# Cutting two value loads of the last head by partitions into 112, 8 and 8 rows, in a transfer-bound decode kernel

## The chip, the cores and the metric

The kernel runs on one core of a Trainium2 chip. The metric is the device time of one execution in microseconds (us). Every run here is in the fast state, and each time is a median; the kernel before was run beside every other kernel on the same chip. The three groups of experiments ran on three different chips; the kernel before differs by 0.07 us between them.

## The reference

One token of decode: layer norm, query projection, attention of 32 heads over a cache of 32,768 keys and values of 192 numbers each (bf16), output projection, then a small feed-forward block.

```python
def _A_ref(x, k_cache, v_cache, wq, wo):
    q = (x @ wq).reshape(B, Sq, 32, 192).transpose(0, 2, 1, 3)
    scores = jnp.einsum("bhqd,bhkd->bhqk", q, k_cache) * (192 ** -0.5)
    o = jnp.einsum("bhqk,bhkd->bhqd", softmax(scores), v_cache)
    return o.transpose(0, 2, 1, 3).reshape(B, Sq, 32 * 192) @ wo
h  = x + A(layernorm(x));   h2 = h + relu(layernorm(h) @ w1) @ w2     # shortened
```

Keys and values are 805 MB which must be read once. Everything else is small beside that.

## The kernel before

All large loads are issued by the sync engine to one queue, in the order in which they are used. A load puts a block of consecutive cache rows on each of 128 partitions:

```python
def load(dst, src, sem, *label):
    g.do(lambda: nc.sync.dma_start(out=dst, in_=src), sem, label, by=16)

def rows(src, h, k0, jl):
    return src[h, k0:k0 + P * jl, :].rearrange("(p j) d -> p (j d)", p=P)
```

The last head is loaded in smaller parts, so that little work is left after the last byte. Below, "the second value load" is the one marked (1), "the half-loads" are (2); J is 32, JL 64, Dh 192, P 128.

```python
        end_values(0, 0, JL * Dh, "dva", "v", LAST, 0)
        ...                                                    # keys
        end_values(1, 0, JL * Dh, "dvb", "v", LAST, 1)         # (1) 128 rows of 24,576 bytes
        ...                                                    # keys: 128 rows of 15,360, 6,144 and 3,072 bytes
        for i in range(2):                                     # (2) 128 rows of 12,288 bytes each
            end_values(2, i * J * Dh, (i + 1) * J * Dh, f"dvh{i}", "vh", i)
        ...                                                    # four last value pieces, wo, w1, w2 in four pieces
```

The softmax here doesn't subtract the row's maximum and nothing guards it: scores larger than these inputs give would overflow.

Of the kernel before, what the change touches and what calls it, by code (L numbers as in the profile page):

```python
# [80 lines left out]
def kernel(  # L81
# [13 lines left out]
    P = nc.NUM_PARTITIONS  # L95

    Bsz, Sq, D = A_x.shape
    _, H, Sk, Dh = A_k_cache.shape
# [9 lines left out]
    JL = 64  # L108
    J = 32
# [6 lines left out]
    LAST = H - 1  # L116
# [31 lines left out]
    v_hd = A_v_cache.rearrange("b h s d -> (b h) s d")  # L148
# [44 lines left out]
    for tag in ("ln1", "ln2"):  # L193
# [16 lines left out]
    v_at = {0: va[:, 0:JL * Dh], 1: va[:, JL * Dh:2 * JL * Dh], 2: va[:, 2 * JL * Dh:3 * JL * Dh],  # L210
            3: va[:, 0:40 * Dh], 4: va[:, 40 * Dh:56 * Dh], 5: va[:, 56 * Dh:64 * Dh]}
# [8 lines left out]
    def v_tile(h, ld):  # L220
        return v_at[ld] if h == LAST else va[:, ld * JL * Dh:(ld * JL + JK) * Dh]
# [11 lines left out]
    def dma_program(g):  # L233
# [6 lines that stand above are left out]
        def keys(h, ld):  # L240
            if h > 0:
                g.wait("PV", h - 1, 4 * ld)
                g.wait("scs", h - 1, 4 * ld + 3)
            elif ld == 1:
                g.wait("att0")
            load(kt[ld][:], rows(k_hd, h, P * JK * ld, JK), f"dk{ld}", "k", h, ld)

        def vals(h, ld):
            if ld == 1:
                g.wait("PV", h, 1)  # L250
            elif h > 0:
                g.wait("PV", h - 1, 5)
            load(v_tile(h, ld), rows(v_hd, h, P * JK * ld, JK), ("dva", "dvb")[ld], "v", h, ld)

        for c in range(DT):
            load(wq_c[c], wq_view[:, c * H * Dh:(c + 1) * H * Dh], f"dwq{c}", "wq", c)
        for h in range(LAST):
            for ld in range(NK):
                keys(h, ld)
                vals(h, ld)  # L260
            if h % 2 == 0 and h < LAST - 1:
                if h > 0:
                    g.wait("prj", h)
                load(wo_s[:], wo_view[h // 2], "dwo", "wo", h // 2)

        def end_keys(i, k0, jl, sem):
            load(k_at[i], rows(k_hd, LAST, k0, jl), sem, "k", LAST, i)

        def end_values(ld, c0, c1, sem, *label):
            load(v_at[ld][:, c0:c1], rows(v_hd, LAST, P * JL * ld, JL)[:, c0:c1], sem, *label)  # L270


        g.wait("PV", LAST - 1, 0)
        g.wait("scs", LAST - 1, 3)
        end_keys(0, 0, JL, "dk0")
        end_keys(1, P * JL, JL, "dke0")
        g.wait("PV", LAST - 1, 3)
        end_values(0, 0, JL * Dh, "dva", "v", LAST, 0)
        g.wait("PV", LAST - 1, 4)
        g.wait("scs", LAST - 1, NC - 1)  # L280
        end_keys(2, 2 * P * JL, JL, "dk1")
        g.wait("PV", LAST - 1, 5)
        end_values(1, 0, JL * Dh, "dvb", "v", LAST, 1)
        k0 = P * JL * (NL - 1)
        at = []
        for i, jl in enumerate(ENDJ):
            at.append((k0, jl))
            end_keys(NL - 1 + i, k0, jl, f"dke{1 + i}")
            k0 += P * jl
        g.wait("PV", LAST - 1, NC - 1)  # L290
        for i in range(2):
            end_values(2, i * J * Dh, (i + 1) * J * Dh, f"dvh{i}", "vh", i)
        i = 0
        for ld, (k0, jl) in enumerate(at):
            for c, (l, off, jc, *_) in enumerate(ends):
                if l == NL - 1 + ld:
                    g.wait("PV", LAST, 1)
                    load(v_tile(LAST, l)[:, off * Dh:(off + jc) * Dh],
                         rows(v_hd, LAST, k0, jl)[:, off * Dh:(off + jc) * Dh], f"dve{i}", "vc", LAST, c)
                    i += 1  # L300
        g.wait("prj", LAST - 1)
        load(wo_s[:], wo_view[H // 2 - 1], "dwo", "wo", H // 2 - 1)
        g.wait("PV", LAST, 3)
        load(w1_s, B_w1.rearrange("(c p) n -> p c n", p=P), "dw1", "w1")
        for i, (c0, c1) in enumerate(zip(W2_CUTS[:-1], W2_CUTS[1:])):
            load(w2_s[:, c0:c1], B_w2.rearrange("(c p) n -> p c n", p=P)[:, c0:c1], f"dw2_{i}", "w2", i)
# [451 lines left out]
    for f in (dma_program, pool_program):  # L758
        f(plan)
# [58 lines left out]
    with nc.Block(name="decode_blk", no_gpsimd_drain=True) as block:  # L818
        @block.sync
        def _(eng):  # L820
            dma_program(Program(book, sems, nc.sync))

        @block.gpsimd
        def _(eng):
            pool_program(Program(book, sems, nc.gpsimd))

        @block.scalar
        def _(eng):
            looped("act", nc.scalar)

        @block.vector
        def _(eng):
            looped("dve", nc.vector)

        @block.tensor
        def _(eng):
            looped("pe", nc.tensor)
# [34 lines left out]
```

## Time and profile before

| | before |
|---|---|
| time, median of 4 | 1914.89 us (1914.77 to 1914.92) |
| busy share of the load queue | 99.8% of 16 engines' span |
| mean rate | 431 GB/s |
| row of 24,576 bytes on one transfer engine | 0.912 us |
| last landing, and end of the profiled span | 1909.35 and 1912.9 us |

In the views PE is the matmul engine, PEld its weight loads, DVE and ACT the vector and scalar engines, POOL is GpSimd and SP the sync engine. The page's views give shares of the span by engine and in 40 slices, the queues, and the chain of waits that ended last. The packet records of the same trace give start, duration and size of each transferred row; I take row durations from there. A full transfer leaves sixteen marks at its landing (the last one's lie within 2.8 us); I take them as one for each of the sixteen engines, and a transfer as landed at its last mark. The lines of the kernel before are shown in the prediction.

### The profile page before, as it was taken

Reading aid. Unit: us, or ns where it says so; the run is one execution under the profiler, and the core shown is the slowest. Engines: PE = TensorE matmul, PEld = TensorE weight load, DVE = VectorE, ACT = ScalarE, POOL = GpSimd, SP = SyncE. Lnnn points to the kernel's source line nnn. Section 1 sums busy time; section 2 is a strip of 40 time slices with the busy share of each in tenths; the row PEclk is TensorE's granted clock in tenths of the full one; section 3 lists DMA queues with packets and bytes.
Section 4 is the critical chain, followed back from the end, with each engine's and each line's share of the span. In section 5 each row is a group of like instructions: output and inputs, shape, how many; then the busy total and the mean of one; then the engine's idle time right before and its main releaser. Section 6 shows DMA issues by size and latency. Waiting matters only on the chain.

```text
span 1912.9 us, 35974 instructions
## 1 busy us (share of the span) xinstructions
PE 1580.2 (83%) x15908; PEld 1000.8 (52%) x15908; DVE 1559.8 (82%) x731; ACT 938.7 (49%) x2001; POOL 1.0 (0%) x6
## 2 busy tenths in 40 slices
PE   7778888888888788888888887878888788888888
PEld 7455455554554555545545545545455455555555
DVE  2787887987878878789788888888798887987887
ACT  2454454554544535545445445455354454553554
POOL 0000000000000000000000000000000000000000
PEclk9988898898898998988989989989889899898899
DMA  9999999999999999999999999999999999999999
GB/s 409 436 433 431 435 432 435 431 439 432 435 432 435 436 430 436 432 436 430 439 432 436 431 436 431 438 432 436 432 435 432 435 433 434 435 430 441 431 429 372
DMA packets 25185, 825.28 MB, mean 431 GB/s; under 512 B 2635, under 2 KB 4172, under 8 KB 7628
## 3 DMA queue, kind: packets, MB, share of 16 engines
q1 hardware_dynamic: 25152, 824.98, 99.8%
q8 instruction: 15, 0.25, 0.0%
q14 instruction: 6, 0.05, 0.0%
q10 hardware_dynamic: 12, 0.00, 0.0%
HBM read 824.97 MB, written 0.00 MB: 431 GB/s over the span
## 4 chain that ended last, share of the span: by engine, by line
DMA 70%; PE 28%; SPq 1%; ACT 1%; issue 0%; POOLq 0%; DVE 0%
DMA va<-in_A_v_cache_dram 69%; PE o_ps L354 25%; PE sp L354 2%; SPq L235 1%; ACT kT L577 1%; PE mm L354 1%; DMA kt<-in_B_w_dram 0%; PE tp L373 0%; POOLq L336 0%; PE attT L354 0%; PE mm L566 0%; ACT pB L583 0%; ACT y_row L639 0%; ACT pA L592 0%; DVE y_col L753 0%
## 5 line engine op out<-in xcount | busy, mean ns | idle before, releaser
L663 DVE TENSOR_TENSOR pr<-kt,qb 128x2304 f32<-128x2304 bf16 (+2 forms) x257 | 755.9, 2941 | 315.3 <-POOLq L317 293.9
L577 ACT COPY kT<-tp 128x1024 bf16<-128x1024 bf16 (+1 forms) x899 | 814.9, 1019 | 286.6 <-PE tp L373 286.5
L666 DVE TENSOR_REDUCE sc<-pr 128x12 f32<-128x2304 f32 (+2 forms) x257 | 755.3, 2939 | 8.9
L354 PE MATMUL o_ps<-va,pB 128*2 128x384 bf16 x2306 | 500.0, 371 | 181.8 <-POOLq L336 147.5
L373 PE MATMUL tp<-ident_f,kt 128*128 128x128 f32 x3459 | 518.5, 288 | 122.7 <-ACT kT L577 75.9
L373 PEld LDWEIGHTS tp<-ident_f,kt 128*128 128x128 f32 x3459 | 380.7, 144 | 222.4 <-ACT kT L577 168.6
L354 PEld LDWEIGHTS o_ps<-va,pB 128*2 128x2 bf16 x2306 | 198.2, 91 | 405.3 <-POOLq L336 152.9
L354 PE MATMUL o_ps<-va,pA 128*2 128x384 bf16 x1790 | 370.6, 352 | 0.0
L592 ACT ACTIVATE pA<-sc 128x12 bf16<-128x12 f32 (+2 forms) x257 | 59.0, 229 | 529.6 <-DVEq L65 529.6
L354 PEld LDWEIGHTS o_ps<-va,pA 128*2 128x2 bf16 x1790 | 161.9, 90 | 173.0 <-issue 54.3
L354 PEld LDWEIGHTS sp<-qm,kT 128*128 128x128 bf16 x6918 | 197.1, 97 | 76.5 <-ACT pB L583 28.4
L354 PE MATMUL sp<-qm,kT 128*128 128x2 bf16 x6918 | 212.6, 164 | 16.2 <-ACT pB L583 13.4
L583 ACT ACTIVATE pB<-sp 128x20 bf16<-128x20 f32 (+2 forms) x258 | 61.4, 238 | 113.0 <-PE sp L354 112.9
L583 ACT ACTIVATION_READ_ACCUMULATOR pB<-sp 128x1 f32 x258 | 64.0, 248 | 0.0
L592 ACT ACTIVATION_READ_ACCUMULATOR pA<-sc 128x1 f32 x257 | 52.9, 206 | 0.0
L354 PE MATMUL o_ps<-xn_ln,kt 128*96 128x1 bf16 (+1 forms) x316 | 22.3, 208 | 2.6 <-DMA kt<-in_A_wq_dram 2.5
L354 PEld LDWEIGHTS o_ps<-xn_ln,kt 128*96 128x96 bf16 (+1 forms) x316 | 22.2, 176 | 2.7 <-issue 2.6
L678 DVE TENSOR_SCALAR o_pair<-o_ps,rec 2x384 bf16<-2x384 f32 x32 | 19.4, 605 | 1.5 <-PE o_ps L354 0.4
L354 PEld LDWEIGHTS attT<-oT,wo_s 128*128 128x128 bf16 x465 | 13.6, 96 | 10.3 <-issue 9.9
L354 PE MATMUL attT<-oT,wo_s 128*128 128x1 bf16 x465 | 16.3, 164 | 0.3 <-DVE oT L688 0.3
L354 PEld LDWEIGHTS mm<-dsums,ones_mat 128*128 128x128 f32 x64 | 9.5, 188 | 10.9 <-issue 10.3
L612 ACT CAST qe<-o_ps 96x64 bf16<-96x64 f32 x1 | 0.2, 208 | 27.5 <-PE o_ps L354 27.5
(65 smaller groups left out, 141.3 us busy)
## 6 DMA issues: line engine op xcount, KB each, us to landing
kt<-in_A_k_cache_dram SPq DMA_DIRECT2D x62, 6144.0 KB, 33.4
va<-in_A_v_cache_dram SPq DMA_DIRECT2D x62, 6144.0 KB, 21.0
kt<-in_A_k_cache_dram SPq DMA_DIRECT2D x3, 3072.0 KB, 24.6
wo_s<-in_A_wo_dram SPq DMA_DIRECT2D x16, 480.0 KB, 15.0
kt<-in_A_wq_dram SPq DMA_DIRECT2D x4, 1536.0 KB, 10.8
va<-in_A_v_cache_dram SPq DMA_DIRECT2D x2, 3072.0 KB, 31.0
va<-in_A_v_cache_dram SPq DMA_DIRECT2D x2, 1536.0 KB, 34.8
kt<-in_A_k_cache_dram SPq DMA_DIRECT2D x1, 1920.0 KB, 30.1
```

The source lines that it names most:

```text
L235: g.do(lambda: nc.sync.dma_start(out=dst, in_=src), sem, label, by=16)
L354: return lambda: pe.matmul(o, lhsT=w, rhs=r, **kw)
L373: calls.append(lambda b=b, o=o: pe.transpose(out=dst[:, b, :], in_=src[:, o:o + 2 * P].bitcast(f32), identity=ident_f[:]))
L577: g.do(lambda: act.copy(out=kT[c % 2][:, b0:b0 + nb, :], in_=src[:, 0:nb, :].bitcast(bf16)), "act_pe", ("cp", h, c, k))
L583: g.do(lambda: act.activation(out=pB[c % NB][:, 0:jp], in_=sp[:, 0:jp], func=F.Exp, scale=SCALE, accum_out=dsums[:, 2 * c + 1:2 * c + 2]), ...
L592: g.do(lambda: act.activation(out=pA[c % NB][:, 0:jd], in_=sc[c % NC][:, 0:jd], func=F.Exp, scale=SCALE, accum_out=dsums[:, 2 * c:2 * c + ...
L612: g.do(lambda: act.copy(out=qe[:], in_=o_ps[0:HE, 0:2 * H]), "act_pe", ("qe",))
L663: g.chain(lambda: dve.tensor_tensor(out=pr[:, 0:j1 - j0, :], in0=src[:, (off + j0) * Dh:(off + j1) * Dh].rearrange("p (j d) -> p j d", d=D ...
L666: g.chain(lambda: dve.reduce_sum(out=sc[c % NC][:, j0:j1], in_=pr[:, 0:j1 - j0, :], axis=X), "dve")
L678: g.do(lambda: dve.tensor_scalar_mul(out=o_pair[:, :, 1, :], in0=o_ps[0:2, 0:2 * Dh].rearrange("q (i d) -> q i d", i=2), scalar1=rec[0:2, ...
```

## The change

If the rows of every load are dealt out evenly, which is the author's premise, all engines' lists are equally long in bytes. Yet the engines do not end together: the marks of the last transfer are spread over 2.8 us. The change is meant to give eight engines, here called 0 to 7, one row more and the others, 8 to 15, one fewer of load (1) and of the first load (2), by cutting off two pieces of eight rows each: 112 rows are counted as seven for each of sixteen engines, a piece as one for each of eight. The traces bear no engine numbers, but they show eight marks for each piece: the page counts 2,667 packets under 512 bytes, the marks among them, after the change and 2,635 before, 32 more for four pieces.

```diff
-        def end_values(ld, c0, c1, sem, *label):
-            load(v_at[ld][:, c0:c1], rows(v_hd, LAST, P * JL * ld, JL)[:, c0:c1], sem, *label)
+        def end_values(ld, c0, c1, sem, *label, cuts=(0, P)):
+            for i, (p0, p1) in enumerate(zip(cuts[:-1], cuts[1:])):
+                load(v_at[ld][p0:p1, c0:c1], rows(v_hd, LAST, P * JL * ld, JL)[p0:p1, c0:c1], sem,
+                     *(label if p1 == P else label + ("part", i)))
+
+        HALF = (0, P - 16, P - 8, P)
...
-        end_values(1, 0, JL * Dh, "dvb", "v", LAST, 1)
+        end_values(1, 0, JL * Dh, "dvb", "v", LAST, 1, cuts=HALF)
...
-            end_values(2, i * J * Dh, (i + 1) * J * Dh, f"dvh{i}", "vh", i)
+            end_values(2, i * J * Dh, (i + 1) * J * Dh, f"dvh{i}", "vh", i, cuts=HALF if i == 0 else (0, P))
```

## The prediction

Port is the author's word here, and in the expectations, for a place in the on-chip memory at which rows of several engines wait for each other. That there are such places was a supposition when this was written. That a row of a piece waits with three others is the premise of the estimates for that case: four times the measured row of 0.912 or 0.460 us.

> **What bounds the kernel now.** I read the page first: busy share by slice, the queues, and the chain that ended last.
>
> ```profile
> PE   7778888888888788888888887878888788888888
> ...
> DMA  9999999999999999999999999999999999999999
> GB/s 409 436 433 431 435 432 435 431 439 432 435 432 435 436 430 436 432 436 430 439 432 436 431 436 431 438 432 436 432 435 432 435 433 434 435 430 441 431 429 372
> ...
> q1 hardware_dynamic: 25152, 824.98, 99.8%
> ...
> DMA 70%; PE 28%; SPq 1%; ACT 1%; issue 0%; POOLq 0%; DVE 0%
> ```
>
> The transfer engines are full in every slice and one queue keeps all sixteen busy for 99.8% of the span, while PE is at 83%. So the time is the time in which the slowest transfer engine empties its list, plus what follows its last byte. The windows of the last head show how near the end that holds (columns: window, its length, busy us and instruction count of PE, weight loads, DVE, ACT, POOL, then granted clock, transfer share, GB/s):
>
> ```profile
> 1860.00:1880.00 20.00, 18.30 (x232) 12.43 (x231) 19.27 (x11) 15.85 (x36) 0.00 (x0) 1.00 0.99 423
> 1880.00:1900.00 20.00, 19.58 (x173) 11.12 (x170) 19.04 (x9) 9.24 (x27) 0.00 (x0) 1.00 1.01 421
> 1900.00:1913.00 13.00, 7.23 (x153) 5.74 (x152) 2.44 (x14) 2.34 (x6) 0.00 (x0) 0.64 0.63 239
> ```
>
> Transfers are saturated until about 1907. Next PE's timeline at the end and the chain in order of time:
>
> ```profile
> 1898.59 1.46 PE L354 MATMUL o_ps<-va,pB 128*2 128x384 bf16 x8 [0.20 <-DMA va<-in_A_v_cache_dram]
> ...
> 1906.99 0.94 PE L354 MATMUL attT<-h1T,kt 128*128 128x1 bf16 x30 [0.75 <-DMA kt<-in_B_w_dram]
> 1908.20 0.56 PE L354 MATMUL attT<-h1T,kt 128*128 128x1 bf16 x15 [0.27 <-DMA kt<-in_B_w_dram]
> 1909.03 0.66 PE L354 MATMUL attT<-h1T,kt 128*128 128x1 bf16 x15 [0.27 <-DMA kt<-in_B_w_dram]
> ```
>
> ```profile
> 1899.56 9.43 DMA kt<-in_B_w_dram
> 1908.98 0.05 issue
> 1909.03 0.67 PE attT L354 x15
> ```
>
> The last value piece, then every piece of w2, is awaited by PE. The last landing is the end, less some 3.5 us of fixed tail (1909.35 to 1912.9). Whatever delays the slowest transfer engine delays the end one for one.
>
> The page does not tell the engines apart, but the trace records sixteen landing marks per transfer. For the last one (last w2 piece) they lie at 1906.54 plus 0, 0.28, 0.69, 0.73, 0.80, 1.12, 1.21, 1.26, 1.35, 1.43, 2.51, 2.62, 2.65, 2.70, 2.72, 2.81 us: ten early engines and six late ones. For the second value load of the last head (mark 1873.59) thirteen lie within 1.43 us and three at 2.65 to 2.83. The pattern is nearly constant from 200 us on, because no engine ever empties: an engine that falls behind stays behind. It changes near instruction blocks: the records show 16,384-byte packets of 0.88 to 0.96 us on the instruction queue at 1865.5, 1875.1, 1887.5 and 1902.2, and after each one more engine lies about 1.3 us later. That is the unevenness which the change would trade against.
>
> [...] The trace shows an engine's own rate (24,576 bytes in 912 ns, 26.9 GB/s) but, with every load spread evenly, nothing of ports shared by engines.
>
> **The change part by part.** No compute instruction moves: the order of PE, DVE, ACT and POOL is the same, and no byte is added. The sync queue has four more issues at 0.33 to 0.43 us each, 1.5 us at most. They are hidden: in the profile it stands blocked at its issues (13.57 us at one of w2) [...]. Four more completion marks at 9 ns each on engines 0 to 7 are nothing.
>
> Rows: a row of the second value load is 24,576 bytes, 912 ns; a row of the first half-load 12,288 bytes, 460 ns. Engines 0 to 7 get one more of each, +1.37 us. Engines 8 to 15 get one fewer of each, -1.37 us.
>
> If all engines run freely, the new end is the larger of (latest of engines 0 to 7, +1.37) and (latest of 8 to 15, -1.37). I cannot see which numbers the six late ones bear. If even one of the latest is in the lower half the end is 1.2 to 1.4 us later. If all six are in the upper half, the lower half is eight of the ten early ones, whose latest is at 1.26 to 1.43; plus 1.37 gives 2.63 to 2.80 against 2.81 now, a gain of 0 to 0.2 us. So with free engines the time is -0.2 to +1.4 us, most likely +1.3: the swap of 2.74 us between the halves overshoots the gap of about 1.3 us, and there was little to win.
>
> If instead the port limits[...]. Four rows through a port take 4 x 0.912 = 3.65 us, not 0.91. Two pieces of the value load take 7.3 us, in place of the one row (0.91) that those engines lose from the 128-row load: +6.4 us. The half-load likewise: 2 x 4 x 0.46 = 3.7 for 0.46, +3.2 us. Sum +9.6 us on engines 0 to 7[...]. It may be more: [...] 5/4 of 7.3 + 3.7 = 13.8, +12.4. The 112-row load may also collide[...]. It is less where the ports have reserve or the collisions overlap with waiting of others. Of the end this makes +8 to +13 us: the transfers before the end are never idle, so nothing hides it, but if the slowest engines were in the upper half up to 2.8 us of their lag is absorbed.
>
> **The rivals.** (a) Free engines, -0.2 to +1.4 us, 1914.7 to 1916.3. For it: [...] no trace here shows a shared port. [...] I give it 35%. (b) Ports shared, +8 to +13 us, 1923 to 1928; 45%. Between both, partial sharing, +2 to +8 us; 15%. (c) A true gain: the late engines are all upper ones and each step waits for them. At most the earlier landing of the six late ones, about 1.3 us, 1913.6; against it the overshoot above; 5%. [...] (e) Compute becomes the bound: PE reaches each awaited piece with 0.2 to 0.75 us of slack, so a gain over about 0.7 us would not pass to the end, and a loss passes fully.
>
> **Range and chances.** Weighted: 0.35 x 0.9 + 0.45 x 10 + 0.15 x 5 - 0.05 x 0.7 = 5.5 us, so 1920.4; the possibilities are in two heaps and I choose the middle between rather than one. The range from 1914.2 to 1927.5 covers (a), the part of (b) up to the estimate with fifth shares, and a bit of gain. Two per cent is 38 us, far outside of all this: within 2% has 0.98.
>
> **What would show it.** Right on shares: the value load's and half-load's small rows last about four times 912 and 460 ns in the packet records, or the landings of the eight-row pieces spread over microseconds; the GB/s of the slices at 1870 to 1890 falls under 400; PE's waits on values and w2 grow by microseconds. Right on free engines: rows keep 912 and 460 ns, and eight landing marks of the last piece move by +1.37 and eight by -1.37 against the others. Wrong altogether if the marks keep their old pattern [...], or if the time falls by over 1 us: then the late engines are the upper eight and the overshoot argument fails.

## The result, and the profile after

The changed kernel takes 1934.21 us (1931.83 to 1937.63 over four runs), against 1914.89. The ratio is 1.0102, with a 95% interval of 1.0085 to 1.012. A ratio here is the mean time of one kernel's fast runs over that of the other's in the same rounds, so it is not quite the ratio of the medians. The change costs 19.3 us. Predicted were 5.5 us (1920.4, with a range up to 1927.5), and within that 8 to 13 us, an estimate, for the case that engines share ports. By the measure of 2% it counts as the same.

The page of the changed kernel, the lines on transfers and the chain:

```profile
DMA  9999999999999999999999999999999999999998
GB/s 415 433 427 434 433 435 433 433 433 433 436 433 433 433 432 436 433 433 433 433 436 433 431 433 434 433 436 431 433 433 434 436 431 433 434 433 437 430 342 283
...
q1 hardware_dynamic: 25184, 824.98, 99.8%
...
DMA 71%; PE 27%; SPq 1%; issue 0%; POOLq 0%; ACT 0%; DVE 0%
```

The busy shares say nothing: the load queue is at 99.8% in both kernels. Only the rate in the last two slices has dropped, from 429 and 372 to 342 and 283 GB/s. So the time by which rows are slowed counts as busy. The windows of the last head show it better (same columns as in the prediction):

```profile
1840.00:1860.00 20.00, 19.38 (x167) 11.57 (x167) 18.68 (x10) 8.34 (x18) 0.00 (x0) 0.93 1.00 433
1860.00:1880.00 20.00, 18.34 (x212) 11.88 (x212) 18.08 (x10) 14.41 (x34) 0.00 (x0) 0.83 1.07 294
1880.00:1900.00 20.00, 10.96 (x72) 5.92 (x72) 16.24 (x8) 3.82 (x11) 0.00 (x0) 0.74 0.94 230
1900.00:1920.00 20.00, 13.48 (x107) 7.05 (x107) 4.00 (x3) 6.95 (x22) 0.00 (x0) 0.83 1.00 352
```

Up to 1860 us nothing differs. Then the transfer share stays about 1 while the rate halves, from 421 to 230 GB/s in the window from 1880 to 1900, and PE's busy time there falls from 19.58 to 10.96 us. PE's timeline shows for what it waits (start, duration, operation, number; in brackets the idle time before it and what ended it):

```profile
1889.04 3.36 PE L358 MATMUL o_ps<-va,pB 128*2 128x384 bf16 x10 [9.11 <-POOLq L340]
...
1906.99 3.36 PE L358 MATMUL o_ps<-va,pB 128*2 128x384 bf16 x10 [6.40 <-DMA va<-in_A_v_cache_dram]
...
1928.58 0.70 PE L358 MATMUL attT<-h1T,kt 128*128 128x1 bf16 x15 [0.28 <-DMA kt<-in_B_w_dram]
```

The first wait is that for the second value load, handed on by GpSimd, which here only relays its landing; the load landed at 1888.94 us. The second is that for the first half-load, whose last mark is at 1906.94 us. The chain in order of time agrees:

```profile
1851.36 37.59 DMA va<-in_A_v_cache_dram
1888.94 0.03 issue
...
1918.02 10.52 DMA kt<-in_B_w_dram
1928.53 0.05 issue
1928.58 0.72 PE attT L358 x15
```

The last landing moves from 1909.35 to 1928.94 us, and the span from 1912.9 to 1932.5: the tail after the last byte keeps its 3.6 us. So the loss lies wholly in the transfers. Here are the rows behind it, from the packet records:

| rows | before, mean us | after, mean us | extra time per engine (rows x difference / 16) |
|---|---|---|---|
| second value load, 128 rows | 0.912 | 1.999 | 8.7 us |
| keys behind it, 128 rows of 15,360 bytes | 0.579 | 0.979 | 3.2 us |
| both half-loads, 256 rows | 0.462 | 0.811 | 5.6 us |

Together they make 17.5 of the 19.6 us by which the last landing moved. The rest is not resolved by this count; engines also end less evenly, over 4.6 us instead of 2.8.

### The profile page after: what moved, and what is told of

Read it like the earlier page. It is cut to its first block, busy times and chain, and to the rows that moved or that the text cites. A ratio compares the mean times of both kernels' runs of the same rounds, so it can differ in the third digit from the quotient of the medians.

```text
span 1932.5 us, 35978 instructions
## 1 busy us (share of the span) xinstructions
PE 1583.9 (82%) x15908; PEld 992.3 (51%) x15908; DVE 1559.8 (81%) x731; ACT 937.5 (49%) x2001; POOL 1.0 (0%) x6
## 2 busy tenths in 40 slices
DMA packets 25217, 825.28 MB, mean 427 GB/s; under 512 B 2667, under 2 KB 4204, under 8 KB 7660
## 3 DMA queue, kind: packets, MB, share of 16 engines
q1 hardware_dynamic: 25184, 824.98, 99.8%
## 4 chain that ended last, share of the span: by engine, by line
DMA 71%; PE 27%; SPq 1%; issue 0%; POOLq 0%; ACT 0%; DVE 0%
DMA va<-in_A_v_cache_dram 70%; PE o_ps L358 24%; PE sp L358 2%; SPq L235 1%; DMA kt<-in_B_w_dram 1%; PE mm L358 1%; POOLq L340 0%; PE tp L377 0%; PE attT L358 0%; PE mm L570 0%; ACT y_row L643 0%; DVE y_col L757 0%; SPq L871 0%; SPq L152 0%
## 5 line engine op out<-in xcount | busy, mean ns | idle before, releaser
L358 PE MATMUL o_ps<-va,pB 128*2 128x384 bf16 x2306 | 508.5, 375 | 199.0 <-POOLq L340 157.7
L377 PE MATMUL tp<-ident_f,kt 128*128 128x128 f32 x3459 | 512.3, 284 | 120.8 <-ACT kT L581 79.3
L377 PEld LDWEIGHTS tp<-ident_f,kt 128*128 128x128 f32 x3459 | 370.9, 142 | 225.5 <-ACT kT L581 175.3
L675 DVE TENSOR_REDUCE rec<-mm 128x1 f32<-128x20 f32 x32 | 5.7, 179 | 21.6 <-PE mm L358 17.1
```

Source lines behind the costliest of these rows:

```text
L358: return lambda: pe.matmul(o, lhsT=w, rhs=r, **kw)
L377: calls.append(lambda b=b, o=o: pe.transpose(out=dst[:, b, :], in_=src[:, o:o + 2 * P].bitcast(f32), identity=ident_f[:]))
L675: g.chain(lambda: dve.reduce_sum(out=rec[:, 0:1], in_=mm[:, 0:2 * NCM], axis=X), "dve")
```

## The experiments

**Theory.** The loads fill the 128 partitions of the on-chip memory. It is supposed that a row waits when another engine writes to partitions that share a port with its own, and that this happens in loads of another shape than 128 rows (rows of 1.999 us in the mean in the changed kernel's second value load), not in a 128-row load (0.912 us). Which partitions share one is for the runs to show: adjacent ones against ones four apart, and the lower 64 against the upper 64. **Rivals.** The uneven lists (nine rows against seven) set the end; each extra transfer costs; the read side, memory, is what collides.

The first two edits are shown against the changed kernel, the others against the kernel before, with the cutting function of the change in place. Twelve kernels ran:

| run | the second value load as | time, us | loss against before of the same rounds |
|---|---|---|---|
| e1_even | 112 and 16 rows; first half-load too | 1931.56 | 16.8 |
| e2_first_only | 112, 8 and 8 rows | 1926.49 | 11.8 |
| e3_halves64 | 64 and 64 rows | 1925.23 | 10.5 |
| e4_columns | three thirds of the columns, 128 rows each | 1914.86 | 0.1 |
| e5_adjacent8 | 16 pieces of 8 adjacent rows | 1945.23 | 30.4 |
| e6_step8 | 16 pieces of 8 rows, 4 partitions apart | 1931.21 | 16.4 |
| e7_adj_to | as e5, source rows four apart | 1952.86 | 38.1 |
| e8_adj_from | as e6, source rows adjacent | 1931.05 | 16.2 |
| e9_seven_apart | 7 times 16 rows, 7 partitions apart; 16 rows | 1925.49 | 10.7 |
| e10_first_even | 112 and 16 rows | 1925.61 | 10.8 |
| e11_adjacent16 | 8 pieces of 16 adjacent rows | 1930.11 | 15.3 |
| e12_shift | 7/8 of the columns whole, 1/8 as 16 pieces of 8 rows, 4 apart | 1917.27 | 2.5 |

The kernel before took 1914.74, 1914.81 and 1914.80 us in the three groups of rounds (e1 to e4, e5 to e8, e9 to e12).

**Are uneven lists the cause?** The first run keeps the 112-row part but gives every engine eight rows.

```diff
-        HALF = (0, P - 16, P - 8, P)
+        HALF = (0, P - 16, P)
```

> Both loads as 112 and 16 rows: every transfer engine keeps eight rows, nobody has nine or seven. Ports theory [...]: the 112-row part stays as slow as in the changed kernel (rows of the second value load 1.5 to 1.8 us instead of 0.91), [...] about two thirds of the loss stays, 1925 to 1932 us. Theory of uneven lists (nine rows against seven delay the end): the loss is gone, 1915 us.

It took 1931.56 us, ratio 1.0091 (1.0074 to 1.0108). With even lists 16.8 of 19.3 us stay, so unevenness is not the main cause. The rows of the 112-row part of the second value load took 1.73 us in the median, as long as in the changed kernel (1.74).

**How much does each load carry?**

```diff
-            end_values(2, i * J * Dh, (i + 1) * J * Dh, f"dvh{i}", "vh", i, cuts=HALF if i == 0 else (0, P))
+            end_values(2, i * J * Dh, (i + 1) * J * Dh, f"dvh{i}", "vh", i)
```

> Only the second value load is cut, the half-load is whole again. Ports theory: the loss follows the bytes that are cut, so two thirds of 19.3 us, about 12 to 13 us, 1927 us. A fixed cost per extra transfer would make it half, 1924.5 us. Uneven lists: 0.92 us of 1.37 us, 1915.8 us.

It took 1926.49 us: 11.8 of 19.3 us, 61%, with the larger of the two cut loads, which has two thirds of their bytes. The remaining 39%, 7.5 us, comes with the half-load. This is nearer to a cost by bytes than to one by transfers, which would be half, but the spread of the changed kernel (5.8 us) is too wide to rule out a mixture by this run alone. The control tests the cost by transfers alone:

```diff
-        end_values(1, 0, JL * Dh, "dvb", "v", LAST, 1)
+        for i in range(3):
+            end_values(1, i * 64 * JL, (i + 1) * 64 * JL, "dvb", *(("v", LAST, 1) if i == 2 else ("v", LAST, 1, "col", i)))
```

> Control: the second value load is cut into three by columns, each with all 128 partitions, so there are as many extra transfers as in the first cut of the change. Ports theory: no collision, 1915 us (within 0.5). A cost per extra transfer, or of shorter runs in memory: several us more.

It took 1914.86 us, ratio 1.0 (0.9984 to 1.0017). Two more transfers and rows a third as long cost nothing that shows. So it is the partitions of a transfer that matter, not the number of transfers.

**Is half of the partitions written at half the rate?**

```diff
-        end_values(1, 0, JL * Dh, "dvb", "v", LAST, 1)
+        end_values(1, 0, JL * Dh, "dvb", "v", LAST, 1, cuts=(0, P // 2, P))
```

> Only the second value load is cut, into partitions 0 to 63 and 64 to 127: four rows an engine from each half, lists even. Ports theory: [...] its 64 rows need 64 x 0.912 / 8 = 7.3 us and the pair 14.6 instead of 7.3 us; rows near 1.82 us each, time 1922 us. Uneven lists or a cost per transfer: 1915 us.

It took 1925.23 us, ratio 1.0053 (1.0036 to 1.007). The windows from 1868 to 1874 us, within the load, of the control by columns and then of this run:

```profile
1868.00:1874.00 6.00, 5.74 (x59) 3.79 (x58) 4.35 (x5) 2.63 (x7) 0.00 (x0) 0.82 1.00 421
```

```profile
1868.00:1874.00 6.00, 3.05 (x40) 2.94 (x39) 5.67 (x6) 1.50 (x6) 0.00 (x0) 0.82 0.98 205
```

The engines are equally busy and move half as much, 205 against 421 GB/s. Rows took 1.89 us in the median; twice 0.912 is 1.82. The loss is larger than the 7.3 us expected (the estimate was half of the partitions at half the rate): eight rows an engine at 1.87 (mean) instead of 0.91 make 7.6 us, and the keys behind it were slowed too, eight rows at 0.83 instead of 0.58, 2.0 us. That engines still at the value load hold them up is my guess; this run does not show it.

**Write side or read side?** The next four runs use 16 pieces of eight rows. The rows of a piece lie on eight adjacent partitions or on eight that are four apart. Destination and source are then exchanged.

```diff
-        end_values(1, 0, JL * Dh, "dvb", "v", LAST, 1)
+        ADJ = [slice(8 * i, 8 * i + 8) for i in range(P // 8)]
+        STEP = [slice(32 * b + r, 32 * b + r + 29, 4) for b in range(P // 32) for r in range(4)]
+        eights(ADJ, ADJ)     # its definition is left out: one load for each pair of slices; (destination, source): e6 (STEP, STEP), e7 (ADJ, STEP), e8 (STEP, ADJ)
```

> Second value load as 16 pieces of eight adjacent rows, half-load whole. [...] Ports theory: [...] 16 pieces 58 us instead of 7.3, so about 1965 us. Uneven lists alone: engines 0 to 7 have 16 rows instead of eight, +7.3 us, 1922 us.

It took 1945.23 us (1941.65 to 1946.88).

> The same 16 pieces of eight rows on engines 0 to 7, but the rows of a piece are four partitions apart[...]. Ports theory: no two rows of a piece collide; 16 x 0.912 = 14.6 instead of 7.3 us [...]: 1922 to 1930 us, some 35 us or more under adjacent rows. Uneven lists or a cost per transfer: the same time as adjacent rows.

It took 1931.21 us (1929.46 to 1932.62). Same number and size of pieces and, by the premise, the same engines and lists, 14.0 us less, though 35 us or more were expected. (The upper end of the expected range, 1930 us, is an estimate for the case that the other eight engines get in the way of some pieces.) Two windows of this run:

```profile
1868.00:1874.00 6.00, 5.84 (x60) 3.86 (x58) 4.09 (x5) 2.78 (x12) 0.00 (x0) 0.86 1.01 422
1876.00:1882.00 6.00, 4.00 (x65) 2.46 (x62) 5.82 (x3) 3.05 (x9) 0.00 (x0) 1.00 1.00 207
```

The first eight pieces belong to partitions 0 to 63: full rate, 422 GB/s, and rows of 0.912 us in the median. The other eight belong to partitions 64 to 127: 207 GB/s, rows of 1.87 us. The marks of the next load fall into two groups of eight here, 1871.05 to 1873.65 and 1894.25 to 1895.28 us. So the small pieces do go to one fixed half of the engines, while the other half is at the next loads. The rows of that other half are slowed too: the first 128 rows of 12,288 bytes, in order of start, which I take as theirs since they run ahead, took 0.94 us in the median instead of 0.46. This is what sharing predicts; a rival by which only the rows of the small pieces are slow would leave them at 0.46. The changed kernel's marks for the second value load agree on the engines: two at the issues of the eight-row pieces (1851.43 and 1851.80 us), then 32 at the landings, which is 16 and twice eight.

> Wrong result on purpose: 16 pieces whose destination is eight adjacent partitions, whose source rows are four apart in memory. If the write side (SBUF ports) is what collides: the time of the run with both adjacent. If the read side (neighbouring rows of memory) collides: the time of the run with both four apart.

It took 1952.86 us, but from 1943.3 to 1959.38 over four runs.

> Wrong result on purpose, the reverse: destination partitions four apart, source rows adjacent. Write side: the time of the run with both four apart. Read side: the time of the run with both adjacent.

It took 1931.05 us (1930.41 to 1931.8), the time of the run with both four apart, within 0.2 us. The destination decides. Whether the source adds something where the destination collides (38.1 against 30.4 us lost) is not settled in view of the spread (1943.3 to 1959.38 against 1941.65 to 1946.88). Both last kernels give value rows to the wrong partitions; the comparison with the reference still passed, so it says nothing here.

With adjacent rows I expected 3.65 us a row, the estimate of four times 0.912, and 51 us of loss; the median row took 2.48 us, and 30.4 us were lost. My guess, which was not tested, is that the eight engines don't stay at the same piece, so that fewer rows wait for each other.

**What does the 112-row part do?** It was the part whose cost the prediction left at zero.

```diff
-        end_values(1, 0, JL * Dh, "dvb", "v", LAST, 1)
+        end_values(1, 0, JL * Dh, "dvb", "v", LAST, 1, cuts=(0, P - 16, P))
```

> The second value load alone as 112 and 16 rows, lists even. Ports theory: two thirds of the loss of the run with both loads so cut (16.8 us), 11 us, 1926 us; against the run with 112 and twice eight rows (1926.5 us) it tells what the two eight-row pieces cost beyond 16 even rows: little. Uneven lists: 1915 us.

It took 1925.61 us (1924.74 to 1926.12), 10.8 us lost. Against it, the two eights of the change cost 0.9 us more (1926.49, in an earlier group on another chip), about the one row, 0.912 us, that engines 0 to 7 have more there; the ranges of the two runs, 1924.74 to 1926.12 and 1925.71 to 1927.84, overlap, so this agrees but does not show it.

```diff
-        end_values(1, 0, JL * Dh, "dvb", "v", LAST, 1)
+        PIECES = [(slice(i, i + 106, 7), 0, JL * Dh) for i in range(7)] + [(slice(P - 16, P), 0, JL * Dh)]
+        first(PIECES)     # its definition is left out: one load for each (partitions, columns)
```

> The second value load alone: 112 rows as seven transfers of 16 rows that lie seven partitions apart, then the last 16 rows[...]. If the single 112-row transfer deals out its rows in that way too, both take about the same time (run with 112 and 16 rows). [...] if the engines stay in step the rows take 0.91 to 1.1 us and the time is 1918 to 1922 us; if being out of step spreads the waiting to all, 1.7 us as in the 112-row load and 1925 us.

It took 1925.49 us (1924.68 to 1925.58), the same as the 112-row load, and its rows took 1.70 us in the median against 1.72. So a 112-row load behaves as if each engine took seven consecutive rows, supposing that a 16-row transfer gives one row to each. (As transfers of 16 adjacent rows, in the run that follows, rows took 2.38 us.) With engines in step I expected 0.91 to 1.1 us, an estimate. None of the first 112 rows, in order of start, was faster than 1.26 us here (1.40 in the changed kernel): no engine is spared the waiting. How it spreads no run tells. A rival is untested: that an engine is slower at any partitions but those that it writes in a 128-row load, even where nobody else writes. So it is shown what the 112-row part costs, but not by which collisions.

```diff
-        end_values(1, 0, JL * Dh, "dvb", "v", LAST, 1)
+        PIECES = [(slice(16 * i, 16 * i + 16), 0, JL * Dh) for i in range(8)]
+        first(PIECES)
```

> The second value load as eight transfers of 16 adjacent rows, one row for each engine, lists even. Ports theory: [...] 3.65 us a transfer in step, 29 instead of 7.3 us, 1937 us; if the engines drift apart as in the run with adjacent eights (rows of 2.5 us), 20 us, 1928 us. Uneven lists, cost per transfer: 1915 us.

It took 1930.11 us (1928.52 to 1931.95), 15.3 us lost, with rows of 2.38 us in the median. It is ordered as expected after the run with 112 and 16 rows, and again milder than the estimate in step (3.65 us).

**Was there a gain in the intent itself?** The last run makes the same shift, nine rows' worth against seven in the second value load, with as few collisions as I could.

```diff
-        end_values(1, 0, JL * Dh, "dvb", "v", LAST, 1)
+        PIECES = [(slice(0, P), 0, 56 * Dh)] + [(slice(32 * b + r, 32 * b + r + 29, 4), 56 * Dh, 64 * Dh)
+                                                for b in range(4) for r in range(4)]
+        first(PIECES)
```

> The intent of the change with the fewest collisions: seven eighths of the columns as one 128-row load, the last eighth as 16 pieces of eight rows four partitions apart on engines 0 to 7. Lists as in the changed kernel's second value load: nine rows' worth on engines 0 to 7, seven on 8 to 15. [...] Uneven lists: engines 0 to 7 end 0.91 us later, so +0.9 us where the late ones are among them, up to +1.9 us with the shared upper ports: 1915.3 to 1916.8 us. If the late engines were all 8 to 15 it would gain up to 0.9 us: 1914.

It took 1917.27 us (1916.03 to 1918.07), ratio 1.0011 (0.9998 to 1.0025). All five runs lie above all nine of the kernel before (1914.63 to 1914.96), though the interval just includes 1. It lost a little more than the 1.9 us expected at most, and gained nothing. The last 48 of its 128 small rows, in order of start, took about 0.2 us instead of 0.12; they belong to the upper 64 partitions. So the waiting at the upper 64 partitions has a part in the 2.5 us, and the cost of the shift alone is not isolated. I ran no version to beat both kernels: if the partitions set the limit, as the runs that exchange destination and source suggest (1952.86 and 1931.05 us), handing their rows to another engine cannot make them end sooner. That is an argument, not a measurement.

## Why the prediction was right or wrong

**What bounds the kernel: right.** The last landing sets the end, one for one, with a fixed tail: 3.6 us in both kernels. The two waits that grew, 9.11 and 6.40 us, are on values, as named beforehand. The waits on w2, which were to grow as well, did not: PE waited 1.3 us for it in three places before, 0.3 us in one place after.

**Hidden issues and extra transfers: right.** Three transfers by columns instead of one cost 0.1 us, and the ranges of the two kernels overlap. (The sum has a slip: four issues at 0.33 to 0.43 us are up to 1.7 us, not 1.5; they took 1.27 us.)

**Which engines take the pieces: right in that they are eight, and the same eight each time.** The two groups of eight marks show it (1871.05 to 1873.65 and 1894.25 to 1895.28 us). **The swap that overshoots: not isolated.** The run that made only the shift was later by 2.5 us, which agrees, but part of that is the waiting at the upper 64 partitions (rows of about 0.2 instead of 0.12 us).

**Rival (a), free engines at 35%: wrong.** Even lists still lose 16.8 us, and equally uneven lists lose 16.4 or 30.4 us as the pieces collide less or more. Rival (b), shared ports, was right for pieces of eight and of 64 rows in that rows wait for each other by where they are written. The runs that exchange destination and source (1952.86 and 1931.05 us), and the run in which both sides slow down (rows of 1.87 instead of 0.912 us, and of 0.94 instead of 0.46), show it. The prediction gave it 45%.

**The eight-row pieces: right in size for the second value load, too dear for the half-load.** Predicted 3.65 us a row; the last 16 rows of that load took 3.58 us in the median. Two of them in place of one of 0.912 make 6.2 us, where the prediction had 6.4. In the half-load a row was to take four times 0.460, 1.84 us; the longest of all 256 rows of 12,288 bytes took 1.38. So at most 2.3 us of the predicted 3.2 can have come true there.

**The term that was mis-sized** is "The 112-row load may also collide". It was put into words and counted as nothing in the sum. Measured: rows of 1.74 us instead of 0.912. Seven of them make 5.8 us more on every engine, in the second value load. Adding this to 6.2 gives 12.0 us, and the run with only that load cut lost 11.8. In the half-load the first 112 rows, in order of start, took 0.86 us instead of 0.46: seven of them make 2.8 us more. So of the 19.3 us, 8.6 us belong to the 112-row parts that the sum left out, and up to 8.5 us (6.2 and at most 2.3) to the eights on which it spent its arithmetic; the rest stays open. The larger part of the transfer, which looked harmless since its lists stayed even, costs about as much as the small pieces. In the run with 112 and 16 rows, where no engine has two eights, seven rows of 1.72 us alone make 5.6 of the 10.8 us lost. Why the 112-row part is slow on every engine stays open, as said above.

**The weighting.** By averaging over two heaps the point, 5.5 us, lay between both, where only the case of partial sharing (15%) was. The range ended at 1927.5 us because the upper end took only the eights into account, with five rows waiting for each other instead of four, an estimate.

## What to carry to other kernels

If transfers are the bound, as here, keep every load at all 128 partitions and cut it by columns: three thirds of the columns cost 0.1 us. A cut by partitions can make rows wait for each other: here it about halved the rate, whether into 64 and 64 rows (205 instead of 421 GB/s from 1868 to 1874 us) or into 112 and 16 (229 GB/s), while pieces of rows four apart on partitions 0 to 63 kept 0.912 us a row. Read GB/s, or the duration of one row, beside the busy share, since the time by which rows are slowed counts as busy (99.8% in both kernels). When a transfer is split, cost the large remainder as well as the small pieces: its rows took 1.74 us here.
